# Small vectors of the input factor on VectorE instead of GpSimd, the weight-column product placed later, and new priorities

## The chip, the cores and the metric

The kernel runs on one core of a Trainium2 chip. The metric is device time in microseconds (us) of one execution; the time before is the median of three runs. One further execution was taken by the profiler, and all rows of the profile below come from it.

## The reference

The input `x` has 2048 rows of 1024. The output mixes two branches with a gate for each row:

```
g = sigmoid((x * gate_w).sum(-1))
a = irfft2(rfft2(x) * (w_r + 1j*w_i))          # a spectral filter over rows and columns
dt = exp(log_dt);  Lam_bar = exp(dt * Lam)      # Lam = Lambda_re + 1j*Lambda_im, 1024 states
B_bar = ((Lam_bar - 1) / Lam)[:, None] * (B_re + 1j*B_im)
h_t = Lam_bar * h_{t-1} + B_bar x_t             # a complex recurrence over the 2048 rows
b = 2 * Re(h @ C.T) + x * Dskip
out = g * a + (1 - g) * b
```

The factor `(Lam_bar - 1) / Lam`, times 2, is the "input factor". It is a complex number for each state: `cr` and `ci` in the kernel.

## The kernel before, in words

Five engines work: TensorE (PE), ScalarE (ACT), VectorE (DVE), GpSimd (POOL) and the DMA queues, above all SyncE's (SP).

The rows come in as 16 tiles of 128 and are turned on PE (`turn`, L476), so that columns lie on partitions (`xT`, four chunks `c` of 512 rows). DVE forms sums and differences of the column halves (`halves`), PE and ACT the reflected part (`xps`, L509 and L511).

The spectral branch then has these steps: `fd`, a transform along columns (L650, L655; copy to SBUF on ACT, L661); `s1`, the first half of the transform along rows (L670, copy L673, a store to DRAM called turn 1); `s2w`, the second half and the product with the weights (L761, copy L764, products on DVE, L767); `is1`, `is2` and `idft` back again (L780, L799, L814). Each runs over 16 tiles. One column of the weights needs a correction: `load_Wc` fetches its pieces, element by element (L693); `fixup_w` makes the weight-column product on PE (L702 to L704) and copies it (L706); `fixup` joins it with the first column of the turn-1 data (`Bcol`, L713 and L719).

The recurrence branch handles 8 blocks `jb` of 128 states and 4 chunks. `bu` multiplies `xT` with the turned matrix B (`psu`, L872), ACT copies this into `h` (L875), DVE rotates it with a table of cosines and sines `cs` (`rot`, L840 to L846), runs the real recurrence as a scan (L884) and, in `rot_out`, rotates back with a table `pn` that also holds the input factor (L840 to L844). `table` makes both tables for a block on ACT and DVE (L619 to L634): its last two ACT instructions (L629, L630) multiply by `ci`, and L631 and L634 on DVE use `cr` and `-cr`. The matrix B of blocks 1 to 7 is turned by DMA (`load_BT`, L859, two buffers).

The output stage `yout` multiplies `h` with C (`ps_y`, L931) and adds the skip term (L938). For row tiles below 12, ACT scales the result (L946) and a DMA issued from POOL adds it to the spectral branch (L947), which `unfold` has put together on DVE (L915, L919); the last four tiles are joined on DVE (L954).

The vectors for the states come from five small rows (`vec8`), turned on PE into `vecT`, 128 x 8 each. From them ACT and DVE make `dt`, the decay `r_sb`, the angle `tht` reduced to one turn `rr2`, and its sine and cosine `sn2`, `cs2` (L544 to L557). In the kernel before, 13 small POOL instructions and four on DVE then make `lbr`, `lbi` and the input factor `cr`, `ci`, `ncr`, and two more on POOL make `ns2`, used where the recurrence passes from chunk to chunk.

The order on every engine is fixed when the program is built. A planner (`Plan.run`) takes all operations with their dependencies, a duration written beside each one, and a key; going forward in its own model of time, it gives each engine the operation that could start first, and among those that could start together the one with the smallest key. A buffer slot also has to be free: PSUM has four slots, the buffers of B two. Some kinds of buffer are given out only in the order in which they were declared, those of B among them. Durations in the plan are `us` arguments such as 0.2 for a small DVE instruction and 0.7 for a small POOL one; a DMA lands in the plan after 0.8 + its duration + 1.4. The keys are written with constants `K_...`:

```
KB = lambda p, cc: K_T0 + K_TB * (p + 0.5 * cc) + K_TL * (p >= 12) + K_TM * (p >= 14)   # psu
KD = lambda p: KB(p, 0) + K_D + K_KR * p + K_D1 * turns[p][1]                           # rotation and scan
KF = lambda j: K_F0 + K_F * j                                                            # fd
KW = lambda b: K_W0 + K_W * b                                                            # s2w
tabs[jb] = table(jb, K_TAB0 if jb == 0 else KB(p, 0) - K_TAB)
load_BT(jb, KB(max(p - 2, 0), 0) + K_BT)
```

`p` runs over 16 turns, a turn being one block and two chunks. The copy of `psu` on ACT has the key of `psu` plus `K_KA`. The result of the plan is a fixed order; at run time each engine works it off and waits wherever something is late.

Of the kernel before, what the change touches and what calls it, by code (L numbers as in the profile page):

```python
# [12 lines left out]
ALU = mybir.AluOpType  # L13
# [10 lines left out]
P = 128  # L24
# [273 lines left out]
def kernel(  # L298
# [17 lines left out]
    nc = tc.nc  # L316
# [66 lines left out]

    U = 0.216
    A2 = nc.scalar.activation
    K_T0 = -22.17
    K_TB = 61.63
    K_D = 1206.47
    K_O = -1656.09
    K_TAB0 = 405.37  # L390
    K_TAB = -79.77
    K_F0 = 60.42
    K_F = 11.71
    K_W0 = -27.89
    K_W = 37.7
    K_WI = -461.38
    K_I0 = -5003.33
    K_I = 60.06
    K_ID = -162.81
    K_CT = 644.51  # L400
    K_FIX = -1360.15
    K_R1 = 3.77
    K_R2 = 2542.1
    K_RS = 59.87
    K_Y = -2627.1
    K_YS = 416.09
# [132 lines left out]
    lbr, lbi, nr, t_a, t_b, t_c, t_d, cr, ci, ncr = [
        small(n) for n in ("lbr", "lbi", "nr", "t_a", "t_b", "t_c", "t_d", "cr", "ci", "ncr")]  # L540
    sv = lambda key, fn, r, w: dve(key, 0.2, fn, r=[(i,) for i in r], w=[(i,) for i in w])
    sa = lambda key, fn, r, w, t=None: act(key, 0.22, fn, r=[(i,) for i in r], w=[(i,) for i in w], table=t)
    sg = lambda key, fn, r, w: pool(key, 0.7, fn, r=[(i,) for i in r], w=[(i,) for i in w])
    sa(1, lambda: A2(out=dt, in_=ldt, func=ACT.Exp), ["vecT"], ["dt"], "exp")  # L544
    sv(2, lambda: V.tensor_mul(out=are, in0=dt, in1=lre), ["dt", "vecT"], ["are"])

# [9 lines left out]
    sa(3, lambda: A2(out=sn2, in_=rr2, func=ACT.Sin, scale=TWO_PI), ["rr2"], ["sn2"], "sin")  # L556
    sa(3, lambda: A2(out=cs2, in_=kk2, func=ACT.Sin, scale=-TWO_PI, bias=chpi), ["kk2", "chpi"], ["cs2"], "sin")  # L557
    cTC, sTC = cs2[:, 1, :], sn2[:, 1, :]
    sv(4, lambda: V.tensor_mul(out=den, in0=lre, in1=lre), ["vecT"], ["den"])
    sv(4, lambda: V.tensor_mul(out=den2, in0=lim, in1=lim), ["vecT"], ["den2"])  # L560
    sv(4, lambda: V.tensor_add(out=den, in0=den, in1=den2), ["den", "den2"], ["den"])
    sv(4, lambda: V.reciprocal(out=inv, in_=den), ["den"], ["inv"])
    sg(4, lambda: G_.tensor_mul(out=lbr, in0=r_sb, in1=cs2[:, 0, :]), ["r", "cs2"], ["lbr"])  # L563
    sg(4, lambda: G_.tensor_mul(out=lbi, in0=r_sb, in1=sn2[:, 0, :]), ["r", "sn2"], ["lbi"])
    sg(4, lambda: G_.tensor_scalar_add(out=nr, in0=lbr, scalar1=-1.0), ["lbr"], ["nr"])
    sg(4, lambda: G_.tensor_scalar_mul(out=inv, in0=inv, scalar1=2.0), ["inv"], ["inv"])
    sg(4, lambda: G_.tensor_mul(out=t_a, in0=nr, in1=lre), ["nr", "vecT"], ["t_a"])
    sg(4, lambda: G_.tensor_mul(out=t_b, in0=lbi, in1=lim), ["lbi", "vecT"], ["t_b"])
    sg(4, lambda: G_.tensor_add(out=cr, in0=t_a, in1=t_b), ["t_a", "t_b"], ["cr"])
    sg(4, lambda: G_.tensor_mul(out=cr, in0=cr, in1=inv), ["cr", "inv"], ["cr"])  # L570
    sg(4, lambda: G_.tensor_mul(out=t_c, in0=lbi, in1=lre), ["lbi", "vecT"], ["t_c"])
    sg(4, lambda: G_.tensor_mul(out=t_d, in0=nr, in1=lim), ["nr", "vecT"], ["t_d"])
    sg(4, lambda: G_.tensor_sub(out=ci, in0=t_c, in1=t_d), ["t_c", "t_d"], ["ci"])
    sg(4, lambda: G_.tensor_mul(out=ci, in0=ci, in1=inv), ["ci", "inv"], ["ci"])
    sg(4, lambda: G_.tensor_scalar_mul(out=ncr, in0=cr, scalar1=-1.0), ["cr"], ["ncr"])
    sg(5, lambda: G_.tensor_copy(out=ns2[:, :, 1], in_=sTC), ["sn2"], ["ns2b"])
# [119 lines left out]
    def fixup_w(key):  # L696
        vps = psum([P, 2, 2, 32], "vps2")

        def f():
            for e in range(2):  # L700
                for i, M in enumerate(((MR, MM), (MN, MR))[e]):
                    mm(vps.t[:, e, i, 1:32], lhsT=fix(M, 0), rhs=Wc[:, e, 1:32], start=True, stop=True)  # L702
# [87 lines left out]
    def is2(bp, key):  # L790
        Cq = tile_of([P, 2, K], BF16, "Cq", "Cq")
        dma(key - K_DM, 0.95, lambda: nc.sync.dma_start(out=Cq.t, in_=t2_v[bp]), r=[("t2", b) for b in range(16)], w=[(Cq,)], issue=0.49)
        psz = psum([P, 4, 2, P], "ps_is2")

        def f():
            for kc in range(4):
                par, half = divmod(kc, 2)
                for gg in range(2):
                    mm(psz.t[:, kc, gg, :], lhsT=Cq.t[:, gg, 256 * half + par:256 * (half + 1):2],  # L799
                       rhs=TI_sb.t[:, bp, :], start=True, stop=True)  # L800
        pe(key, 0.65, f, r=[(Cq,), (TI_sb,)], w=[(psz,)])
        ZT = tile_of([P, 4, 2, P], BF16, "ZT", "ZT")
        act(key, 1.01, lambda: nc.scalar.copy(out=ZT.t, in_=psz.t), r=[(psz,)], w=[(ZT,)])  # L803
        return ZT
# [248 lines left out]
```

## Time and profile before

| what | value |
|---|---|
| median of three runs | 327.17 us (326.19 to 328.23) |
| the profiled execution | 326.46 us |
| its span | 324.6 us |
| PE busy | 307.5 us, 95% |
| DVE busy | 284.1 us, 88% |
| ACT busy | 204.7 us, 63% |
| POOL busy | 36.1 us, 11% |

The span is the time from the first to the last instruction of the profiled execution, and 1.86 us of its own time lie around it. A share of busy time is a mean over stages: ACT has little to do in the last 120 us and is full before. A line of the order of time gives the start, the length, the engine, the source line, what is written and read, and in brackets how long the engine was idle before and what ended this.

### The profile page before, as it was taken

To read this page: it belongs to the slowest core of one execution; us is meant where nothing else is said; L and a number is where in the kernel's file an instruction comes from. 1 tells how busy PE (TensorE), PEld (TensorE's weight loads), DVE (VectorE), ACT (ScalarE), POOL (GpSimd) and SP (SyncE) were. 2 spreads that over 40 slices of the span, in tenths; PEclk is the share of its full clock that TensorE was granted. 3 is DMA by queue.
4 is the path that set the end of the run, shared out by engine and by line. 5 is a ranking of instruction groups with operands and counts; after the bars stand their busy time and mean duration, and the time that the engine had idled before them with its cause. 6 is when DMAs were issued, how large, how long until landed. Compare 5 with 4: busy or idle time off the path is not lost.

```text
span 324.6 us, 5143 instructions
## 1 busy us (share of the span) xinstructions
PE 307.5 (95%) x1836; PEld 165.8 (51%) x1869; DVE 284.1 (88%) x439; ACT 204.7 (63%) x280; POOL 36.1 (11%) x47
## 2 busy tenths in 40 slices
PE   5978899999999999999999999999999999999994
PEld 5644665665444444444476566545444444554442
DVE  3999699999999999999899999999999999904114
ACT  3698699999899999989999998304000222131000
POOL 1137300000000000000000000000000444534000
PEclk9999999999999999999999999999999999999999
DMA  7969326997979999985889999770000787896203
GB/s 227 398 156 68 65 98 175 229 223 187 212 194 292 249 294 298 218 225 100 221 195 216 283 243 274 168 269 17 0 0 2 130 179 174 182 175 124 77 0 129
DMA packets 79409, 56.51 MB, mean 174 GB/s; under 512 B 49684, under 2 KB 65428, under 8 KB 79384
## 3 DMA queue, kind: packets, MB, share of 16 engines
q1 hardware_dynamic: 75848, 53.03, 62.8%
q0 software_dynamic: 3456, 3.15, 8.8%
q8 instruction: 14, 0.23, 0.3%
q14 instruction: 11, 0.09, 0.1%
q10 hardware_dynamic: 80, 0.01, 0.0%
HBM read 28.38 MB, written 16.79 MB: 139 GB/s over the span
## 4 chain that ended last, share of the span: by engine, by line
PE 54%; DVE 18%; ACT 16%; DMA 5%; issue 3%; POOL 3%; DVEq 0%; ACTq 0%
PE psu L872 24%; PE ps_y L931 15%; DVE h L884 7%; DMA ga<-y 4%; DVE h L841 3%; ACT h L875 3%; POOL lbr L563 2%; PE ps_id L814 2%; DVE su L840 2%; PE pt L476 2%; DVE h L842 2%; PE ps_fd L650 2%; PE ps_s L670 2%; PE ps_s L761 2%; PE ps_is L780 2%
## 5 line engine op out<-in xcount | busy, mean ns | idle before, releaser
L872 PE MATMUL psu<-xT,BTs 128*128 128x512 bf16 x498 | 115.8, 379 | 2.8 <-ACT G_all L673 0.5
L931 PE MATMUL ps_y<-CT,h 128*128 128x512 bf16 x499 | 112.7, 379 | 1.5 <-ACT y L946 0.8
L872 PEld LDWEIGHTS <-BTs 128*128 128x128 bf16 x512 | 49.6, 98 | 59.1 <-issue 2.7
L931 PEld LDWEIGHTS <-h 128*128 128x128 bf16 x512 | 49.3, 98 | 57.2 <-issue 1.1
L884 DVE TENSOR_TENSOR_SCAN h<-r_sb,carry,h 128x512 bf16<-128x512 f32 x48 | 60.0, 1272 | 0.0
L946 ACT ACTIVATE y<-ps_y,omg 128x512 f32<-128x512 f32 x24 | 15.7, 685 | 69.4 <-PE ps_y L938 32.8
L947 POOL DMA_DIRECT2D ga<-y x24 | 21.3, 1290 | 241.7 <-DVE ga L919 235.7
L875 ACT CAST h<-psu 128x1024 bf16<-128x1024 f32 x32 | 33.3, 1044 | 0.9 <-PE psu L872 0.6
L842 DVE TENSOR_TENSOR h<-h,su 128x1024 bf16<-128x1024 bf16 (+1 forms) x40 | 23.1, 576 | 0.2
L841 DVE TENSOR_TENSOR h<-h,pn 128x1024 bf16<-128x1024 bf16 (+1 forms) x24 | 20.7, 862 | 0.1
L840 DVE TENSOR_TENSOR su<-h,pn 128x1024 bf16<-128x1024 bf16 (+1 forms) x24 | 20.6, 857 | 0.0
L841 DVE TENSOR_TENSOR h<-h,cs 128x2048 bf16<-128x2048 bf16 x16 | 19.6, 1223 | 0.4
L840 DVE TENSOR_TENSOR su<-h,cs 128x2048 bf16<-128x2048 bf16 x16 | 19.3, 1206 | 0.0
L884 DVE TENSOR_TENSOR_SCAN h<-r_sb,h 128x512 bf16<-128x512 f32 x16 | 18.9, 1210 | 0.0
L819 ACT ACTIVATE M_all<-ps_id,gA 128x1024 bf16<-128x1024 f32 x14 | 16.6, 1235 | 2.7 <-PE ps_id L814 2.7
L764 ACT CAST h<-ps_s 128x1024 bf16<-128x1024 f32 x16 | 15.8, 1023 | 0.6 <-remote 0.5
L784 ACT CAST h<-ps_is 128x1024 bf16<-128x1024 f32 x16 | 15.6, 1016 | 0.0
L803 ACT CAST M_all<-ps_is 128x1024 bf16<-128x1024 f32 x14 | 15.3, 1127 | 0.2 <-PE ps_is L799 0.2
L954 DVE SCALAR_TENSOR_TENSOR o<-ps_y,omg,ga 128x1024 bf16<-128x1024 f32 (+1 forms) x5 | 5.3, 1070 | 11.5 <-issue 9.7
L814 PE MATMUL ps_id<-G_all,M_all 128*128 128x256 bf16 x112 | 14.1, 273 | 0.5 <-ACT M_all L803 0.5
L919 DVE TENSOR_TENSOR ga<-G_all 128x512 bf16<-128x512 bf16 x16 | 6.0, 420 | 9.5 <-DMA out_dram<-ga 9.5
L476 PE MATMUL pt<-ident,xn 128*128 128x128 bf16 x128 | 10.0, 242 | 4.0 <-DMA xn<-in_A_x_dram 3.5
(141 smaller groups left out, 413.5 us busy)
## 6 DMA issues: line engine op xcount, KB each, us to landing
xn<-in_A_x_dram SPq DMA_DIRECT2D x16, 256.0 KB, 4.9
h<-turn_scratch SPq DMA_DIRECT2D x16, 256.0 KB, 5.3
turn_scratch<-h SPq DMA_DIRECT2D x16, 256.0 KB, 2.9
ga_scratch<-M_all SPq DMA_DIRECT2D x14, 256.0 KB, 4.3
M_all<-ga_scratch SPq DMA_DIRECT2D x6, 512.0 KB, 4.4
ga<-y POOLq DMA_DIRECT2D x24, 128.0 KB, 5.9
out_dram<-ga SPq DMA_DIRECT2D x12, 256.0 KB, 2.1
turn_scratch<-M_all SPq DMA_DIRECT2D x11, 256.0 KB, 4.9
```

Of the source, the lines that this page charges most:

```text
L476: nc.tensor.transpose(out=pt.t[:, j8, :], in_=src()[:, P * j8:P * (j8 + 1)], identity=ident)
L764: act(key, 1.01, lambda: nc.scalar.copy(out=X2.t, in_=ps2.t), r=[(ps2,)], w=[(X2,)])
L814: mm(pz.t[:, at, :], lhsT=ZT.t[:, 2 * par + half, c, :], rhs=Gi_sb[:, par, half, c, :], start=(half == 0), stop=(half == 1))
L819: act(key, 1.11, lambda: A2(out=eo.t, in_=pz.t, func=ACT.Copy, scale=gA[:, bp:bp + 1]), r=[(pz, 0), (pz, 1), ("gA",)], w=[(eo,)])
L840: dve(key, w, lambda: nc.vector.tensor_mul(out=sv(), in0=src()[:, ::-1], in1=bc(1)), r=sitem + [titem(1)], w=[(su,)])
L841: dve(key, w, lambda: nc.vector.tensor_mul(out=dst(), in0=src(), in1=bc(0)), r=sitem + [titem(0)], w=ditem)
L842: dve(key, h, lambda: nc.vector.tensor_add(out=dst()[:, 0], in0=dst()[:, 0], in1=sv()[:, 0]), r=[(su,)] + r0, w=r0)
L872: mm(psu.t[:, ri, :], lhsT=BT.t[:, ri, db, :], rhs=xT[c][:, db, :], start=(db == 0), stop=(db == 7))
L875: act(kb[cc] + K_KA, 1.01, lambda cc=cc, psu=psu: nc.scalar.copy(out=g()[:, :, cc, :], in_=psu.t), r=[(psu, 0), (psu, 1)], w=ui(cc) + ([(" ...
L884: dve(kd, 1.25, lambda cc=cc, ri=ri, carry=carry: nc.vector.tensor_tensor_scan(out=g()[:, ri, cc, :], data0=rb, data1=g()[:, ri, cc, :], i ...
L931: mm(psy.t[:, 512 * dh:512 * (dh + 1)], lhsT=hbuf[jb // 4].t[:, jb % 4, ri, P * tb:P * (tb + 1)], rhs=CT[pc].t[:, ri, jb % 2, 512 * dh:512 ...
L947: dma(key - 1, 1.3, lambda cols=cols, y32=y32: nc.gpsimd.dma_start(out=ga.t[:, tb % 2, cols], in_=y32.t, accum_op=ALU.add), r=[(y32,)] + [ ...
```

## The change

The products that make the input factor are written with pairs: `cr` and `ci`, real and imaginary part, lie beside each other in one tile, and most instructions handle both. All run on DVE, so that POOL has no part in them. `fixup_w` is called after the loop of `s1`, gets a key of its own, and waits for the turn-1 store of tile 8. The planned duration of the `is2` product goes from 0.65 to 0.46. All key constants have new values, and the small vectors get an offset `K_SM`.

```
-    K_T0 = -22.17
-    K_TB = 61.63
-    K_D = 1206.47
-    K_TAB0 = 405.37
-    K_TAB = -79.77
-    K_F0 = 60.42
-    K_F = 11.71
-    K_W0 = -27.89
-    K_W = 37.7
-    K_R2 = 2542.1
-    K_BT = 425.36
-    K_UN = 2960.8
-    K_KA = -0.82
-    K_WC = 261.15
+    K_T0 = 91.34
+    K_TB = 75.5
+    K_D = 1883.45
+    K_TAB0 = -249.3
+    K_TAB = -891.13
+    K_F0 = 225.83
+    K_F = 11.93
+    K_W0 = -3238.17
+    K_W = 5.91
+    K_R2 = 2615.95
+    K_BT = -266.03
+    K_UN = 3245.96
+    K_KA = 503.92
+    K_KR = -45.15
+    K_WC = 148.64
+    K_FW = -2495.45
+    K_SM = -5128.56
...
-    sv = lambda key, fn, r, w: dve(key, 0.2, fn, ...)
-    sa = lambda key, fn, r, w, t=None: act(key, 0.22, fn, ...)
-    sg = lambda key, fn, r, w: pool(key, 0.7, fn, ...)
+    cs2, sn2 = trig[:, 0], trig[:, 1]
+    sv = lambda key, fn, r, w: dve(key + K_SM, 0.2, fn, ...)
+    sa = lambda key, fn, r, w, t=None: act(key + K_SM, 0.22, fn, ...)
...
-    sv(4, lambda: V.tensor_mul(out=den, in0=lre, in1=lre), ...)
-    sv(4, lambda: V.tensor_mul(out=den2, in0=lim, in1=lim), ...)
-    sv(4, lambda: V.tensor_add(out=den, in0=den, in1=den2), ...)
-    sv(4, lambda: V.reciprocal(out=inv, in_=den), ...)
-    sg(4, lambda: G_.tensor_mul(out=lbr, in0=r_sb, in1=cs2[:, 0, :]), ...)
-    sg(4, lambda: G_.tensor_mul(out=lbi, in0=r_sb, in1=sn2[:, 0, :]), ...)
...
-    sg(4, lambda: G_.tensor_mul(out=ci, in0=ci, in1=inv), ...)
-    sg(4, lambda: G_.tensor_scalar_mul(out=ncr, in0=cr, scalar1=-1.0), ...)
-    sg(5, lambda: G_.tensor_copy(out=ns2[:, :, 1], in_=sTC), ...)
-    sg(5, lambda: G_.tensor_scalar_mul(out=ns2[:, :, 0], in0=sTC, scalar1=-1.0), ...)
+    lam = vecT[:, 0:2, :]
+    two = lambda v: v[:, None, :].to_broadcast([P, 2, 8])
+    cr, ci = co[:, 0, :], co[:, 1, :]
+    sv(4, lambda: V.scalar_tensor_tensor(out=sq, in0=lam, scalar=0.5, in1=lam, op0=ALU.mult, op1=ALU.mult), ...)
+    sv(4, lambda: V.tensor_add(out=inv, in0=sq[:, 0, :], in1=sq[:, 1, :]), ...)
+    sv(4, lambda: V.reciprocal(out=inv, in_=inv), ...)
+    sv(4, lambda: V.tensor_mul(out=lb, in0=trig[:, :, 0, :], in1=two(r_sb)), ...)
+    sv(4, lambda: V.tensor_scalar_add(out=lb[:, 0, :], in0=lb[:, 0, :], scalar1=-1.0), ...)
+    sv(4, lambda: V.tensor_mul(out=lb, in0=lb, in1=two(inv)), ...)
+    sv(4, lambda: V.tensor_mul(out=m1, in0=lb, in1=lam), ...)
+    sv(4, lambda: V.tensor_mul(out=m2, in0=lb, in1=lam[:, ::-1, :]), ...)
+    sv(4, lambda: V.tensor_add(out=cr, in0=m1[:, 0, :], in1=m1[:, 1, :]), ...)
+    sv(4, lambda: V.tensor_sub(out=ci, in0=m2[:, 1, :], in1=m2[:, 0, :]), ...)
+    sv(4, lambda: V.tensor_scalar_mul(out=ncr, in0=cr, scalar1=-1.0), ...)
+    sv(5, lambda: V.tensor_copy(out=ns2[:, :, 1], in_=sTC), ...)
+    sv(5, lambda: V.tensor_scalar_mul(out=ns2[:, :, 0], in0=sTC, scalar1=-1.0), ...)
...
-        pe(key, 0.6, f, r=[("Wc", n) for n in range(8)] + [(TF_sb,)], w=[(vps,)])
+        pe(key, 0.6, f, r=[("Wc", n) for n in range(8)] + [(TF_sb,), ("t1", 8)], w=[(vps,)])
...
-        pe(key, 0.65, f, r=[(Cq,), (TI_sb,)], w=[(psz,)])
+        pe(key, 0.46, f, r=[(Cq,), (TI_sb,)], w=[(psz,)])
...
-    fixup_w(60)
     X1 = fd(0, KF(0))
     for j in range(16):
         nxt = fd(j + 1, KF(j + 1)) if j + 1 < 16 else None
         s1(j, X1, KF(j + 1) + 1)
         X1 = nxt
+    fixup_w(K_FW)
     fixup(K_FIX)
```

More of the change, by code (lines that the diff above doesn't have):

```diff
@@ L533, in small @@
         return cpool.tile([P] + list(shape), FP32, name=n)
-    V, G_ = nc.vector, nc.gpsimd
-    dt, are, r_sb, den, den2, inv = [small(n) for n in ("dt", "are", "r_sb", "den", "den2", "inv")]
-    tht, kk2, rr2, sn2, cs2 = [small(n, (2, 8)) for n in ("tht", "kk2", "rr2", "sn2", "cs2")]
+    V = nc.vector
+    dt, are, r_sb, inv, ncr = [small(n) for n in ("dt", "are", "r_sb", "inv", "ncr")]
+    tht, kk2, rr2, sq, lb, m1, m2, co = [small(n, (2, 8)) for n in ("tht", "kk2", "rr2", "sq", "lb", "m1", "m2", "co")]
+    trig = small("trig", (2, 2, 8))
     ns2 = small("ns2", (8, 2))
[L539 to L543, printed above, removed]
+    cs2, sn2 = trig[:, 0], trig[:, 1]
+    sv = lambda key, fn, r, w: dve(key + K_SM, 0.2, fn, r=[(i,) for i in r], w=[(i,) for i in w])
+    sa = lambda key, fn, r, w, t=None: act(key + K_SM, 0.22, fn, r=[(i,) for i in r], w=[(i,) for i in w], table=t)
     sa(1, lambda: A2(out=dt, in_=ldt, func=ACT.Exp), ["vecT"], ["dt"], "exp")
@@ L558 @@
     cTC, sTC = cs2[:, 1, :], sn2[:, 1, :]
[L559 to L576, printed above, removed]
@@ new lines @@
+    sv(4, lambda: V.tensor_mul(out=lb, in0=trig[:, :, 0, :], in1=two(r_sb)), ["r", "cs2", "sn2"], ["lb"])
+    sv(4, lambda: V.tensor_scalar_add(out=lb[:, 0, :], in0=lb[:, 0, :], scalar1=-1.0), ["lb"], ["lb"])
+    sv(4, lambda: V.tensor_mul(out=lb, in0=lb, in1=two(inv)), ["lb", "inv"], ["lb"])
+    sv(4, lambda: V.tensor_mul(out=m1, in0=lb, in1=lam), ["lb", "vecT"], ["m1"])
+    sv(4, lambda: V.tensor_mul(out=m2, in0=lb, in1=lam[:, ::-1, :]), ["lb", "vecT"], ["m2"])
+    sv(4, lambda: V.tensor_add(out=cr, in0=m1[:, 0, :], in1=m1[:, 1, :]), ["m1"], ["cr"])
```

61 lines of the change are left out of this document (33 added, 28 removed).

## The prediction

> **What bounds the kernel now.** I read the busy totals first, then the busy time in stretches of 10 us, then the waits of each engine, then the order of time where the waits lie, and last the end.
>
> ```profile
> PE 307.5 (95%) x1836; PEld 165.8 (51%) x1869; DVE 284.1 (88%) x439; ACT 204.7 (63%) x280; POOL 36.1 (11%) x47
> ```
>
> ```profile
> 10.00:20.00 10.00, 9.04 (x110) 6.82 (x109) 9.82 (x23) 7.55 (x11) 2.57 (x3) 1.00 1.06 375
> 20.00:30.00 10.00, 8.68 (x38) 3.61 (x37) 9.89 (x17) 9.86 (x15) 5.65 (x5) 1.00 0.67 18
> 30.00:40.00 10.00, 7.91 (x59) 5.51 (x61) 7.22 (x9) 5.48 (x8) 5.21 (x9) 1.00 0.49 93
> 40.00:50.00 10.00, 9.41 (x58) 6.08 (x58) 9.97 (x14) 9.97 (x13) 0.00 (x0) 1.00 0.31 106
> ...
> 170.00:180.00 10.00, 9.45 (x79) 6.55 (x79) 9.93 (x13) 10.00 (x12) 0.00 (x0) 1.00 1.04 228
> ...
> 270.00:280.00 10.00, 9.95 (x47) 4.54 (x47) 10.00 (x17) 0.18 (x1) 4.43 (x6) 1.00 0.79 160
> ```
>
> ```profile
> 3.54 3.60 PE L476 MATMUL pt<-ident,xn 128*128 128x128 bf16 x32 [3.54 <-DMA xn<-in_A_x_dram]
> ...
> 319.77 0.61 PE L938 MATMUL ps_y<-diag,xT 128*128 128x128 bf16 x8
> ```
>
> The columns after each stretch are the busy us of PE, PEld, DVE, ACT and POOL, the granted clock (1.00), the DMA share and GB/s. TensorE is idle 324.6 - 307.5 = 17.1 us in all. It starts at 3.5 us and its last product ends at 320.4, 4.2 us before the end, so about 9.3 us is idle inside, and that is all that any reordering can win. The hole is early: 20 to 40 us lacks 1.32 + 2.09 us. After 40 us DVE is as full as PE (10.00 of 10), and around 170 us ACT is too. Three engines are near their limits, so a gain in one counts only if the others come along.
>
> The waits (engine and line, what it waited for, us in total, times, longest):
>
> ```profile
> ACT tt L629 <- POOL ci L574: 4.0, 1, 4.0
> DVE pn L631 <- ACT tt L629: 3.6, 2, 2.7
> PE ps_s L670 <- ACT M_all L661: 1.4, 1, 1.4
> PE vps L702 <- DMA Wc<-in_A_w_i_dram: 0.9, 1, 0.9
> PE ps_y L931 <- ACT y L946: 0.8, 1, 0.8
> PE psu L872 <- ACT G_all L673: 0.5, 1, 0.5
> PE ps_id L814 <- ACT M_all L803: 0.5, 1, 0.5
> PE psu L872 <- ACT M_all L819: 0.4, 1, 0.4
> PE psu L872 <- ACT h L875: 0.4, 1, 0.4
> PEld L719 <- DMA Bcol<-turn_scratch: 0.4, 1, 0.4
> ```
>
> In order of time (start, length, engine and line):
>
> ```profile
> 10.06 0.16 DVE L545 TENSOR_TENSOR are<-dt,vecT 128x8 f32<-128x8 f32 x1
> 10.14 0.16 DVE L547 TENSOR_TENSOR tht<-dt,vecT 128x8 f32<-128x8 f32 x1
> ...
> 18.28 0.21 ACT L556 ACTIVATE sn<-rr 128x16 f32<-128x16 f32 x1
> ...
> 25.62 0.38 ACT L557 ACTIVATE cs<-kk,chpi 128x16 f32<-128x16 f32 x1
> ...
> 26.08 7.52 POOL L563 TENSOR_TENSOR lbr<-r_sb,cs 128x8 f32<-128x8 f32 x1 [4.35 <-ACT cs L557]
> ...
> 35.29 0.20 POOL L574 TENSOR_TENSOR ci<-ci,inv 128x8 f32<-128x8 f32 x1
> ...
> 37.64 1.22 DVE L840 TENSOR_TENSOR su<-h,cs 128x2048 bf16<-128x2048 bf16 x1
> ```
>
> So the early hole is one chain. The cosines come at 26.0, because their ACT instruction (key 3) stood behind the transposes' copies, whose keys are negative. Then POOL takes 7.52 us for one 128x8 product that takes it 0.20 us elsewhere, `ci` is there at 35.5, ACT has stood 4.0 us before `tt` L629, and DVE 2.7 us before `pn` L631. The fd copies (L661) queued behind on ACT, and so `ps_s` L670 and `psu` L872 on PE waited 1.4 and 0.5 us.
>
> **The change, part by part.**
>
> *Small vectors.* Fifteen POOL instructions and four DVE ones go; thirteen DVE ones come. Their price is read from L545 and L547: each lasts 0.16 us, but starts 0.08 us after the one before. DVE gains 13 - 4 = 9 instructions, 9 x 0.08 = 0.72 us; the other end is 9 x 0.16 = 1.44 us. I take 0.72, since these run in a full queue as those two did. It lies on DVE ahead of the halves that fd needs; PE has psu products to do meanwhile. If that cover were gone, it would cost 0.72. Against it stand the 2.7 us that DVE no longer waits for `pn`: its first rotation (L840, 37.64) should come 2.7 - 0.7 = 2.0 us earlier.
>
> The Trainium skill, "VectorE: DVE Perf Modes", section on the TRN2 errata, speaks against such a move: every VectorE instruction on SBUF pays a fixed latency, which its formula puts at (8 + 151)/0.96 = 166 ns here, and many small ones pay it each time. By that the nine would cost 1.5 us and the rotation would come 1.2 us earlier; the 0.16 us lengths agree with it, the 0.08 us steps do not.
>
> *Keys K_SM and K_TAB0.* K_SM = -5128 puts the whole chain, its ACT parts too, ahead of all copies and halves. The chain began at 10.06 with `are`; sines came 8.2 us later only because of what was queued between. I expect `cs` before 18.3 and `ci` by 22, where 35.5 was. Table 0 (K_TAB0 405 to -249) follows at once. The new wait is that DVE itself now stands before `lb` until ACT has made `cs`; behind it in the same queue are the copies of xT and the halves, and behind these fd on PE. DVE had 0.2 us of slack from 10 to 20 us, so lateness there moves fd, but PE still has psu of jb 0. Bounds: 0 to 1.3 us (half of the 2.7 won); I take 0 for the end.
>
> ACT's 4.0 us hole is then used by what is next in its queue (fd copies, the table of jb 1). So `ps_s` 1.4 and `psu` 0.5 on PE go: 1.9 us. Bounds 1.0 and 1.9; I take 1.9, because both waits name the copies queued behind L629.
>
> *The weight-column product.* Removed: its 0.9 us wait on PE for Wc. It is now placed after the eighth turn-1 store has landed. PE's order is written down by the planner, which allows that store 0.8 + 0.85 + 1.4 = 3.05 us.
>
> ```profile
> turn_scratch<-M_all SPq DMA_DIRECT2D x11, 256.0 KB, 4.9
> ...
> 13.71 8.94 SPq L693 DMA_DIRECT2D Wc<-in_A_w_r_dram  x4
> ...
> 26.98 2.12 SPq L859 DMA_TRANSPOSE BTs<-in_B_B_re_dram  x1
> 29.16 1.29 SPq L859 DMA_TRANSPOSE BTs<-in_B_B_im_dram  x1
> ```
>
> The store lands after 4.9, 1.85 us late, and all later products queue behind the wait. The nearest row of a product placed behind a DMA by the same rule is L719 behind Bcol, 0.4 us of wait. Bounds 0 and 1.85; I take 0.4, net gain 0.5. The twelve products themselves are unchanged.
>
> *BT loads.* K_BT from +425 to -266 puts jb 1's key at 91 - 266 = -175, below every x tile; but its buffer may be taken only after BTb[0] (the slots are taken in order), by which time x is issued. So the two transposes go on SP before TF and TK, or G too, and before the Wc loads instead of behind them: issued near 12 to 16 us instead of 27.0 to 30.5. G, TF and Wc go 2.1 + 1.3 = 3.4 us later; fd and s1 need G and TF only after 34 us, so 0. It gives PE psu work for 30 to 41 us that it lacked; that is the cover for fd's later start, counted at 0 (0 to 1.0, the rest of the early hole).
>
> *The other keys.* The order in each stage is set by differences, which I compared. fd 226 to 405 against psu 91 + 75.5 p: nearly the old place. s2w and is1, is2 and idft stay ahead of psu. Rotations to chunks 2 and 3 stay behind most scans (2616 on, the last scan's key is 2906). New is K_KA = +504: psu's copy on ACT goes behind all fd and s1 copies. I hold this at 0 and carry it as a rival. With ACT some 4 us ahead, the three waits of PE for ACT near 165 to 185 us (0.5, 0.4, 0.4) should shrink: bounds 0 and 1.3. I take 1.3, the whole of it, since each is a third of what ACT is ahead or less.
>
> **The sum.** 1.9 + 0.5 + 1.3 = 3.7 us for PE. DVE must follow:
>
> ```profile
> 277.20 0.68 DVE L844 TENSOR_TENSOR h<-su,h 128x1024 bf16<-128x1024 bf16 x1
> ...
> 281.24 0.61 PE L938 MATMUL ps_y<-diag,xT 128*128 128x128 bf16 x8
> ```
>
> The last rotation ends at 277.9; PE then uses it in the eight products before 281.24 (about 1.7 us), from 279.5. So PE has 1.6 us over DVE, and DVE comes 2.0 earlier: PE can win 3.6 at most without new waits. I take 3.6. The profiled execution took 326.46 us (span 324.6), 0.71 under the median of 327.17, inside the runs' 326.19 to 328.23. It becomes 326.46 - 3.6 = 322.9; from the median 323.6, which is the forecast, 1.1% below. About 1% is what a measurement here can tell from no change, 3.3 us.
>
> **The rivals.**
>
> *A. Given back at the end.* Output tiles leave PSUM through ACT into buffers that a POOL-issued addition must empty, and these additions wait for the unfold on DVE; PE already waited 0.8 us there (`ps_y` L931).
>
> ```profile
> 253.67 6.46 DMA ga<-y
> 260.21 0.69 ACT y L946
> ...
> 261.77 5.71 DMA ga<-y
> ```
>
> If PE reaches the tiles 3.6 us earlier and the unfold does not, since its key rose from 2961 to 3246 against scans that end at 2906, then PE waits for the same additions. For: two such flights lay on the chain that ended last. Against: DVE comes 2.0 earlier. Price 2.0 to 3.6, so 326.4.
>
> *B. Slower: copies of psu starve PE.* There are four PSUM tiles. In the fd stage (about 38 to 77 us) ACT makes 32 fd and s1 copies, about 0.90 us apart, 29 us, for which PE does 16 x (0.87 + 0.43) = 20.8 us of products. If psu's copies (keys 595 on) get no turn against keys of 226 to 417, two or more tiles are stuck and PE loses up to 29 - 20.8 = 8.2 us there.
>
> ```profile
> 60.36 1.04 ACT L673 CAST G_all<-ps_s 128x1024 bf16<-128x1024 f32 x1
> 61.26 1.05 ACT L661 CAST G_all<-ps_fd 128x1024 bf16<-128x1024 f32 x1
> ...
> 58.34 0.60 PE L650 MATMUL ps_fd<-G_all,xpm 128*128 128x256 bf16 x4
> 58.78 0.60 PE L655 MATMUL ps_fd<-G_all,xpm 128*128 128x256 bf16 x4
> 59.22 0.38 PE L670 MATMUL ps_s<-M_all,TF_sb 128*128 128x512 bf16 x1
> ```
>
> Time 327.17 - 3.6 + 8.2 = 331.8. It decides from a loss above 3.6 + 3.3 = 6.9 us for over 1% slower. For: ACT is full in that stage. Against: s1's copy needs s1's product, which needs fd's copy, so ACT has gaps in which psu is next; and where the spectral copies already went first (170 to 180 us) PE lost only 0.55 in 10.
>
> *C. More than forecast.* If the new order also fills most of what is left of the 9.3 us, 6.5 us goes: 320.7. Against: DVE would have to win 4.9.
>
> *D. The change does nothing* to the end, since DVE's 0.7 us and the late store eat the gain: 327.2, counted with A.
>
> **How the numbers follow.** Forecast 0.46 (own range 321.8 to 325.4, two thirds of it under 323.9, since 3.6 is the DVE limit and the order itself may add), A with D 0.24, B 0.20, C 0.10. Faster by over 1%: 0.10 + 0.32 = 0.42. Within 1%: 0.14 + 0.24 = 0.38. Slower: 0.20. The range 319.8 to 330.5 takes in C, A and the milder half of B, and leaves out some 0.16.
>
> **What would show it.** Right: no POOL product after the start, `ci` by 22 us; ACT's 4.0 us and DVE's 2.7 us waits gone; first L840 near 35.6; PE busy over 19 of the 20 us from 20 to 40; the weight-column product between s1 products with a wait below 0.5. A is right if PE's wait before `ps_y` L931 near 260 grows to 3 us; B if PE falls below 9 in 10 between 40 and 80 us while ACT is at 10. The forecast is wrong if the early waits go and the span does not shrink by 2 us, or if `lb` holds DVE for over 1.3 us.

## The result, and the profile after

The changed kernel takes 325.37 us (median of 20 runs, 324.40 to 327.45) against 326.86 us of the kernel before (median of 20, 325.81 to 329.44): ratio 0.9949, 95% interval 0.9929 to 0.9968. That is 1.67 us less by the ratio (1.0 to 2.3), less than half of the 3.6 us that were forecast. The profiled execution has a span of 323.2 us, 1.4 less than before's 324.6.

The busy time of TensorE in stretches of 10 us, columns as in the prediction, shows the early hole filled:

```profile
10.00:20.00 10.00, 8.70 (x105) 6.50 (x103) 9.96 (x31) 8.00 (x13) 0.00 (x0) 1.00 1.17 328
20.00:30.00 10.00, 8.87 (x42) 3.91 (x41) 9.88 (x17) 10.00 (x15) 0.00 (x0) 1.00 0.79 101
30.00:40.00 10.00, 10.00 (x61) 6.20 (x60) 9.86 (x14) 8.81 (x13) 0.00 (x0) 1.00 0.34 53
40.00:50.00 10.00, 9.93 (x67) 6.82 (x65) 10.00 (x14) 10.00 (x12) 0.00 (x0) 1.00 0.49 149
```

From 20 to 40 us TensorE is idle for 1.13 us instead of 3.41, and from 40 to 50 for 0.07 instead of 0.59. Against that, 10 to 20 us loses 0.34, by a new wait at 17.7 us (below). The early stage gives 2.28 + 0.52 - 0.34 = 2.46 us.

Two late stretches, first before, then after:

```profile
160.00:180.00 20.00, 18.92 (x165) 13.38 (x167) 19.93 (x31) 20.00 (x24) 0.00 (x0) 1.00 0.96 224
180.00:200.00 20.00, 19.41 (x151) 12.86 (x152) 19.88 (x29) 20.00 (x29) 0.00 (x0) 1.00 1.06 263
260.00:280.00 20.00, 19.07 (x94) 8.84 (x95) 20.00 (x32) 3.44 (x5) 7.95 (x10) 1.00 0.83 171
```

```profile
160.00:180.00 20.00, 18.10 (x162) 12.56 (x159) 19.97 (x33) 19.98 (x24) 0.00 (x0) 1.00 0.99 236
180.00:200.00 20.00, 19.22 (x147) 12.00 (x145) 19.86 (x30) 18.88 (x26) 0.00 (x0) 1.00 1.04 265
260.00:280.00 20.00, 20.00 (x101) 9.28 (x99) 20.00 (x32) 1.26 (x2) 7.04 (x8) 1.00 0.80 157
```

From 160 to 200 us TensorE is idle for 2.68 us instead of 1.67: 1.0 us is lost where 1.3 was to be won. Around 267 us the wait for an output tile's copy is gone, 0.93 us won that no term of the sum held. Together 2.46 - 1.01 + 0.93 = 2.4 us. Before's trace lacks 33 matmul records, so such differences of busy time are a little uncertain; the last product of TensorE is the better witness:

```profile
317.81 0.61 PE L936 MATMUL ps_y<-diag,xT 128*128 128x128 bf16 x8
```

It ends at 318.42 us, 1.96 earlier than before. From there to the end 4.78 us pass instead of 4.22, with the same work on VectorE between (the last row of VectorE ends 1.5 us after TensorE in both), so the difference lies in the last stores of one execution.

What TensorE still waits for in the changed kernel (us in total, times, longest):

```profile
...
PE pt L478 <- ACT xT L481: 1.3, 2, 1.1
PE psu L870 <- ACT M_all L513: 1.1, 1, 1.1
PE ps_id L812 <- ACT G_all L801: 0.9, 2, 0.6
PE ps_id L812 <- ACT M_all L801: 0.8, 1, 0.8
PE psu L870 <- ACT G_all L817: 0.6, 1, 0.6
PE psu L870 <- ACT M_all L817: 0.4, 1, 0.4
```

The waits for `ps_s`, for Wc and for `ps_y` are not in it. Two early waits are new. At 17.7 us `pt` waits 1.1 us for a copy of `xT` that now stands on ScalarE behind a table load and the small sines and cosines (15.0 to 16.7 us, where K_SM puts them). By this trace it is a price of the early place; no run took it away. At 25.9 us psu waits 1.1 us. The other rows lie between 163 and 197 us. The chain that filled the early hole, in order of time:

```profile
12.55 1.55 SPq L857 DMA_TRANSPOSE BTs<-in_B_B_re_dram  x1
14.15 4.33 SPq L857 DMA_TRANSPOSE BTs<-in_B_B_im_dram  x1
...
16.43 0.29 ACT L558 ACTIVATE trig<-kk,chpi 128x16 f32<-128x16 f32 x1
...
18.61 0.17 DVE L572 TENSOR_TENSOR co<-m 128x8 f32<-128x8 f32 x1
...
23.58 0.75 ACT L627 ACTIVATE tt<-tf,co 128x512 f32<-128x512 f32 x1
...
36.77 1.22 DVE L838 TENSOR_TENSOR su<-h,cs 128x2048 bf16<-128x2048 bf16 x1
```

The cosines come at 16.4 instead of 25.6 us, `ci` at 18.8 instead of 35.5, ScalarE's scaling of the table starts at 23.6 without a wait, and the B loads of block 1 run at 12.6 to 18.5 us.

### The profile page after: what moved, and what is told of

Its sections match the earlier page's. It is cut to its first block, busy times and chain, and to the rows that moved or that the text cites. A ratio compares the mean times of both kernels' runs of the same rounds, so it can differ in the third digit from the quotient of the medians.

```text
span 323.2 us, 5180 instructions
## 1 busy us (share of the span) xinstructions
PE 308.9 (96%) x1869; PEld 165.3 (51%) x1869; DVE 285.2 (88%) x448; ACT 204.6 (63%) x280; POOL 22.5 (7%) x32
## 4 chain that ended last, share of the span: by engine, by line
PE 62%; ACT 17%; DMA 9%; DVE 6%; issue 3%; SPq 2%; DVEq 0%; ACTq 0%
PE ps_y L929 34%; PE psu L870 14%; PE ps_id L812 2%; DMA wA<-in_A_w_r_dram 2%; PE ps_y L936 2%; ACT h L782 2%; ACT M_all L801 2%; PE ps_fd L648 2%; PE ps_fd L653 2%; PE ps_s L668 2%; DVE wA L765 1%; ACT h L873 1%; DMA Bcol<-turn_scratch 1%; DMA wB<-in_A_w_i_dram 1%; DMA xn<-in_A_x_dram 1%
## 5 line engine op out<-in xcount | busy, mean ns | idle before, releaser
L873 ACT CAST h<-psu 128x1024 bf16<-128x1024 f32 x32 | 32.4, 1022 | 3.0 <-PE psu L870 3.0
L882 DVE TENSOR_TENSOR_SCAN h<-r_sb,h 128x512 bf16<-128x512 f32 x16 | 18.8, 1208 | 0.0
L817 ACT ACTIVATE M_all<-ps_id,gA 128x1024 bf16<-128x1024 f32 x12 | 13.6, 1162 | 1.0 <-PE ps_id L812 1.0
L801 ACT CAST M_all<-ps_is 128x1024 bf16<-128x1024 f32 x12 | 12.6, 1060 | 1.3 <-PE ps_is L797 1.3
L812 PE MATMUL ps_id<-G_all,M_all 128*128 128x256 bf16 x96 | 12.4, 273 | 0.8 <-ACT M_all L801 0.8
```

What stands on the lines that cost most here:

```text
L812: mm(pz.t[:, at, :], lhsT=ZT.t[:, 2 * par + half, c, :], rhs=Gi_sb[:, par, half, c, :], start=(half == 0), stop=(half == 1))
L873: act(kb[cc] + K_KA, 1.01, lambda cc=cc, psu=psu: nc.scalar.copy(out=g()[:, :, cc, :], in_=psu.t), r=[(psu, 0), (psu, 1)], w=ui(cc) + ([(" ...
L882: dve(kd, 1.25, lambda cc=cc, ri=ri, carry=carry: nc.vector.tensor_tensor_scan(out=g()[:, ri, cc, :], data0=rb, data1=g()[:, ri, cc, :], i ...
```

## The experiments

Two kinds of kernel were run. In the first, each engine's order is written down, as the kernel before has it or as the changed kernel has it, and one thing is moved in it. In the second, the planner draws up the order anew. All come from one source with other line numbers: L988 is the product psu and L991 its copy; L587 the copy of xps, L777 that of fd, L786 the s1 product, L818 the weight-column product; L919 and L935 are the copies of the inverse stage (the changed kernel's L801 and L817), L915 and L930 its products ps_is and ps_id; L960 is the last step of a rotation; L1035 the additions of the unfolding, L1063 the additions that POOL issues, L1047 and L1054 the output products and L1062 their copy; L745 and L747 are the table's scaling by `ci` and its use in `pn`. The kernel before, measured again beside them, took 326.9 to 327.5 us, so kernels are compared by their ratios to it.

| kernel | us | ratio to before | 95% interval |
|---|---|---|---|
| bo_dve | 326.36 | 0.9982 | 0.9961 to 1.0004 |
| bo_vps | 328.31 | 1.0042 | 1.0023 to 1.0060 |
| bo_both | 326.21 | 0.9976 | 0.9957 to 0.9994 |
| bo_both_unf | 326.09 | 0.9964 | 0.9943 to 0.9985 |
| bo_both_unf2 | 325.67 | 0.9940 | 0.9913 to 0.9967 |
| ao_pool | 324.84 | 0.9945 | 0.9918 to 0.9971 |
| ao_pool_late | 330.23 | 1.0097 | 1.0065 to 1.0129 |
| ao_dve_late | 328.54 | 1.0039 | 1.0013 to 1.0066 |
| ao_diag | 324.83 | 0.9929 | 0.9907 to 0.9952 |
| ao_light | 324.01 | 0.9894 | 0.9868 to 0.9920 |
| oldkeys_newcode | 355.51 | 1.0858 | 1.0829 to 1.0888 |
| newkeys_is2_065 | 327.36 | 1.0003 | 0.9985 to 1.0020 |

### The edits in the order of before

**bo_dve**: the small vectors alone.

```diff
 order of before
-POOL: lbr, lbi, nr, inv, t_a, t_b, cr, ... ncr, ns (15), behind the cosines
+DVE:  ns, lb, lb-1, lb*inv, m1, m2, cr, ci, ncr (10), behind the last subtraction before the cosines
```

> The order of the kernel before is kept on every engine, instruction by instruction; only the small vectors are made in pairs on VectorE, the ten that need the cosine directly behind the subtraction that DVE did at 26.9 us. Theory 1 (the early chain is what the change removes, and the gain reaches the end): ACT's wait of 4.0 us before L629 and DVE's 2.7 us before L631 go, the first rotation comes near 35.6 instead of 37.6, PE wins 1.4 + 0.5 us near 40, and since nothing else moves the whole rest shifts: 1.5 to 2.0 us faster, ratio near 0.995. Theory 2 (the gain is one of the new order, the small vectors were hidden): the early waits shrink, later waits grow by as much, ratio 1.000 within 0.001.

```profile
PE ps_y L1047 <- ACT y L1062: 1.5, 1, 1.5
PE vps L818 <- DMA Wc<-in_A_w_i_dram: 1.5, 1, 1.5
```

The waits of 1.4 us for `ps_s` and of 0.5 for psu are gone or down to 0.2, 1.7 us won. But Wc is now waited for 1.5 us instead of 0.9, since TensorE reaches that product earlier and the load lands when it did, and the output tile's copy at 267 us 1.5 instead of 0.8. So 1.3 of 1.7 is given back. The ratio is 0.18% below 1, and its interval takes in 1. This is rival A of the prediction, in the old order.

**bo_vps**: the weight-column product alone.

```diff
 order of before
-PE vps, ACT Vc   (at 30.6 us)
+PE vps, ACT Vc   directly ahead of zps
```

> The order of the kernel before is kept; only the twelve small weight-column products and their copy are moved to just before the first-column products (L719, 85 us). POOL still makes the small vectors. Theory 1: PE's 0.9 us wait for Wc goes, but fd then meets the same late ACT (L629), so the gain is 0 to 0.9 us, ratio 0.997 to 1.000. Theory 2: 1.000 within 0.001.

TensorE in order of time (the bracket holds the idle time before, and what ended it), then busy time and granted clock (the seventh number) in two stretches:

```profile
39.00 0.59 PE L786 MATMUL ps_s<-M_all,TF_sb 128*128 128x512 bf16 x2 [2.72 <-ACT M_all L777]
...
41.41 1.06 PE L786 MATMUL ps_s<-G_all,TF_sb 128*128 128x512 bf16 x2
```

```profile
38.00:40.00 2.00, 1.00 (x7) 0.75 (x7) 1.97 (x2) 2.00 (x4) 0.00 (x0) 1.00 0.00 0
40.00:42.00 2.00, 2.00 (x9) 1.13 (x8) 1.97 (x4) 2.00 (x3) 0.00 (x0) 0.53 0.00 0
```

The 0.9 us at Wc turns into 1.3 us more in front of `ps_s`, because POOL's slow `ci` still sets when that is fed. On top of it the clock falls to half from 40.1 us, 1.1 us after the wait has ended, and a like pair of s1 products takes 1.06 instead of 0.59 us. Both theories missed: the edit alone costs 0.42%.

**bo_both**: the two together.

> The order of the kernel before with both edits at once: small vectors on VectorE and the weight-column products at 85 us. Theory 1: the early waits of PE, 0.9 + 1.4 + 0.5 = 2.8 us, go together, and 2.0 to 2.8 us reach the end, ratio 0.991 to 0.994, as good as the changed kernel (0.995) or better, with no new priorities. Theory 2: the changed kernel stays ahead; this one is at 0.998 to 1.000.

```profile
PE ps_fd L766 <- DVE xpm L574: 0.7, 2, 0.5
...
PE ps_y L1047 <- ACT y L1062: 1.1, 1, 1.1
```

0.24% is won, close to what the second theory says. What stands in the way is VectorE's later halves (`xpm`, 0.7 us) and again the end.

**bo_both_unf** and **bo_both_unf2**: is the wait at the end what eats the gain?

```diff
 VectorE's order of bo_both
 bo_both_unf:
-ga additions 2 to 4 of the first pair at 248.2 to 251.2 us
+ga additions 2 to 4 of the first pair at 233.8 us
 bo_both_unf2, that and:
-pq and ga, six additions of the second pair, between rotations at 252.7 to 261 us
+the six together ahead of the rotation at 253.3 us
```

> Both edits in the kernel before's order, as in the earlier run of it (326.2 us, ratio 0.9976), and now three additions of the first unfolded pair (`ga`, on VectorE at 248.2 to 251.2 us there) placed at 234 us. Theory 'given back at the end': there TensorE waits 1.1 us at 267 us for an output tile's copy, which waits for a buffer, which waits for a POOL-issued addition, which waits for those three. Then the wait falls under 0.3 us and the time by about 1.1 us to 325.1, ratio near 0.994. Rival 'VectorE sets the end': three additions of 0.42 us ahead of rotations make TensorE wait for the rotations, 326.2 or up to 327. Rival 'the next wait takes its place': the y wait goes, another of 1 us appears, 326.2.

> Both edits in the order of before, and the first two unfolded pairs' additions on VectorE earlier: three of the first pair at 234 us (which alone left the wait at 267 us as it was, since the copy there waits for the POOL additions at 260 us, and these for the second pair), and the six of the second pair together at 253.3 to 256 us instead of 252.7 to 261. Theory 'given back at the end': POOL's additions come some 5 us earlier, TensorE's wait of 1.1 us at 267 us falls under 0.3, the time falls by 0.8 to 1.1 us to 325.2 (ratio near 0.9945, as the change). Rival 'VectorE sets the end': the rotation behind the six comes 1.3 us later and TensorE waits for it instead, 326.2 or more.

The first one missed: the wait stayed at 1.1 us, since the copy at 267 us hangs on POOL's second group of additions, at 260.6 us, and that on the second pair. In bo_both_unf2 that group is issued at 255.9:

```profile
255.92 3.52 POOL L1063 DMA_DIRECT2D ga<-y  x4 [17.15 <-issue]
```

```profile
268.36 11.61 PE L1047 MATMUL ps_y<-CT,h 128*128 128x512 bf16 x52 [0.21 <-DVE h L960]
```

Now 0.2 us is left, and that is for a rotation. The ratio is 0.9940, as the whole change has it (0.9949). So rival A's wait was real: the trace shows it gone, the span falls from 324.3 us in bo_both to 323.6, and the two edits in the old order then give what the change gives. The ratios of bo_both and bo_both_unf2 alone do not separate the two, since their intervals overlap.

### The engine, or the place

**ao_pool**: the changed kernel's order with the fifteen POOL instructions back, at the early place.

```diff
 order of the changed kernel
-DVE:  ns, lb, ... ncr (10) at 16.6 to 18.9 us
+POOL: the 15 instructions of before, behind the cosines at 16.8 us
```

> The order of the changed kernel is kept; only the small vectors go back to POOL, where they start behind the cosine at 16.7 us. Theory 1 (it is the late input factor that costs): one of the fifteen POOL products stands still for some 5 to 8 us again, ci comes at 25 to 29 us instead of 18.7, ACT waits before L627 (23.6 us) for 2 to 5 us, and 1 to 2 us of the gain are lost: ratio 0.998 to 1.002. Rival: the early place alone is what counts; POOL is done by 23 us and the ratio stays near 0.995.

```profile
17.86 0.20 POOL L680 TENSOR_TENSOR lbr<-r_sb,cs 128x8 f32<-128x8 f32 x1
...
19.75 0.74 POOL L691 TENSOR_TENSOR ci<-ci,inv 128x8 f32<-128x8 f32 x1
```

`lbr` took 7.52 us before and takes 0.20 here, and the time is the changed kernel's (0.9945 against 0.9949). The second theory holds: it is the early place (K_SM) that counts, not VectorE.

**ao_pool_late** and **ao_dve_late**: the cosines late again.

```diff
 order of the changed kernel, small vectors on POOL or on DVE
-ACT cs at 16.4 us, small vectors behind it
+ACT cs and small vectors directly ahead of ACT's scaling of the table (23.6 us)
```

> The changed kernel's order with the small vectors on POOL (as fast as the changed kernel when the cosines come at 16.8 us), and now cosines and small vectors only right before the table's scaling by `ci` (about 23.9 us). Theory 'place, not engine': the cosines then fall among VectorE's products of two operands in SBUF (23.0 to 27 us), the first POOL product takes several us instead of 0.20, `ci` comes near 30, ScalarE waits 4 us or more, and TensorE loses 1 to 3 us: 326 to 328. Rival 'length of the chain only': each product 0.20 us, `ci` at 27.5, ScalarE waits some 3 us, the time within 0.5 us of after's 325.4.

> The changed kernel's order with cosines and small vectors (on VectorE, in pairs, as in the change) only right before the table's scaling by `ci` (about 23.9 us). Theory 'place, not engine': VectorE waits some 0.3 us for the cosines, the ten small instructions take 1.1 to 1.4 us, ScalarE waits about 1.3 us for `ci`; the time within 0.5 us of after's 325.4, and below the same place on POOL by 1 us or more. Rival 'the early place is all': as slow as on POOL in that place.

On POOL:

```profile
23.88 0.57 POOL L680 TENSOR_TENSOR lbr<-r_sb,cs 128x8 f32<-128x8 f32 x1 [6.23 <-ACT cs L674]
```

```profile
27.30 0.72 ACT L745 ACTIVATE tt<-tf,ci 128x512 f32<-128x512 f32 x1 [3.50 <-POOL ci L691]
```

```profile
29.58 9.75 PE L988 MATMUL psu<-xT,BTs 128*128 128x512 bf16 x31 [4.93 <-ACT M_all L587]
```

```profile
30.00:32.00 2.00, 2.00 (x6) 0.70 (x5) 2.00 (x4) 2.00 (x4) 0.00 (x0) 0.50 0.41 1
```

On VectorE, the ten instructions' first and last, and TensorE behind them:

```profile
24.19 0.17 DVE L649 COPY ns<-trig 128x8 f32<-128x8 f32 x1
...
25.36 0.17 DVE L648 TENSOR_SCALAR ncr<-co 128x8 f32<-128x8 f32 x1
```

```profile
27.79 8.75 PE L988 MATMUL psu<-xT,BTs 128*128 128x512 bf16 x31 [2.65 <-ACT M_all L587]
```

Both missed. No POOL product took several us: the first four took 0.48 to 0.57, the others 0.20, so ScalarE waited 3.5 us for the length of the chain. Yet the times are far beyond what either theory gave: 330.2 and 328.5. The wait on TensorE is 4.9 us (2.65 with VectorE) where the changed kernel has 1.1, and behind it the 32 products of psu, of which these traces hold 31, take 9.75 us (8.75). In the changed kernel the same ones take 7.07:

```profile
25.89 7.07 PE L870 MATMUL psu<-xT,BTs 128*128 128x512 bf16 x32 [1.13 <-ACT M_all L513]
```

So 3.8 us of wait and 2.7 of a slow clock (1.5 and 1.7) make 6.5 us (3.2); the spans, 329.0 and 326.7, are 5.8 and 3.5 above the changed kernel's. In this place VectorE beats POOL by 1.7 us, which is what the change of engine is worth when the chain is late.

### The late waits

**ao_diag** and **ao_light**: what ScalarE does from 160 to 200 us.

```diff
 ScalarE's order of the changed kernel
 ao_diag:
-eight diag copies at 178.9 to 192.5 us
+eight diag copies behind the last copy of the inverse stage (205 us)
 ao_light, that and:
-two scalings of the last table at 173.0 and 175.4 us (pn on DVE at 173.9 and 176.8)
+two scalings at 205 us (pn on DVE at 208.7)
-psu copy at 195.1 us, then the copy for ps_id
+the copy for ps_id, then the psu copy
```

> The changed kernel's order with one thing moved: the eight small ScalarE copies that make the diagonal (some 0.3 us each, 2.4 us, at 178.9 to 192.5 us) go behind the last copy of the inverse stage (205 us), where ScalarE stands idle. Theory 'ScalarE is the bound from 160 to 200 us': it is at 10.00 of 10 there, so 2.4 us less work ends TensorE's waits after 179 us (0.78 at 197 us), TensorE idle from 180 to 200 us falls from 0.78 to below 0.3, the time falls by 0.5 to 0.8 us to 324.7; the waits from 163 to 178 us (1.9 us) stay. Rival 'each wait is the length of one copy that the next product needs, whatever the load': waits and time stay as after's, 325.4. Rival 'VectorE sets the end': the waits go and the time does not.

> The changed kernel's order with ScalarE's work put off where TensorE waits for it: besides the eight diagonal copies (moved to 205 us, which alone moved no wait), the two scalings of the last table (at 173.0 and 175.4 us, 1.6 us, used only after 206 us) go to 205 us with their two VectorE instructions behind them, and one copy of psu (195.1 us) goes behind the copy of the inverse stage that TensorE waits for at 197 us. Theory 'ScalarE's local order': each late wait of TensorE is a copy that queued behind an instruction nobody needed yet. Then the waits of 0.57 us at 177 and 0.78 at 197 us go, those of 0.63 at 163 and 0.40 at 167 us stay, TensorE gains about 1.3 us and the time falls to 324.0, ratio near 0.9905. Rival 'VectorE sets the end': TensorE's waits go and others for VectorE come, 325.2. Rival 'one copy's length': the waits stay, 325.2.

Busy time in ao_diag, then in ao_light:

```profile
180.00:200.00 20.00, 19.11 (x150) 12.53 (x151) 19.89 (x29) 17.12 (x19) 0.00 (x0) 1.00 1.11 257
```

```profile
160.00:180.00 20.00, 18.39 (x163) 12.85 (x164) 19.93 (x32) 19.29 (x21) 0.00 (x0) 1.00 0.98 226
180.00:200.00 20.00, 19.83 (x153) 12.85 (x153) 19.86 (x30) 17.56 (x20) 0.00 (x0) 1.00 1.06 253
```

In ao_diag ScalarE has 1.8 us less to do from 180 to 200 us and TensorE waits as before (0.89 idle), so that "ScalarE is full there" is not the cause of the waits. The time went to 324.83 us, near the expected 324.7, but the ratios (0.9929 and the change's 0.9949) are not apart by their intervals, and the waits that this fall was to come from did not change. In ao_light, which moves what stands directly ahead of the copies that TensorE waits for, 180 to 200 us lacks only 0.17 us, and the whole stretch from 160 lacks 1.78 instead of 2.68. The wait of 0.8 us at 197 us is gone; that at 177 shrank from 0.57 to 0.35 only. At 197 us ScalarE and TensorE stood so in the changed kernel, then in ao_light:

```profile
195.07 1.03 ACT L873 CAST h<-psu 128x1024 bf16<-128x1024 f32 x1
195.97 1.03 ACT L801 CAST M_all<-ps_is 128x1024 bf16<-128x1024 f32 x1
...
197.06 1.05 PE L812 MATMUL ps_id<-G_all,M_all 128*128 128x256 bf16 x8 [0.78 <-ACT M_all L801]
```

```profile
194.01 2.11 ACT L919 CAST M_all<-ps_is 128x1024 bf16<-128x1024 f32 x2
...
195.07 2.16 PE L930 MATMUL ps_id<-G_all,M_all 128*128 128x256 bf16 x16
```

The copy for `ps_id` no longer stands behind the copy of psu, and TensorE's products follow without a gap.

The time goes to 324.01, ratio 0.9894, whose interval does not touch the change's; the expected 324.0 was met. It is the fastest kernel of this study, 0.55% (1.8 us) below the changed kernel by the two ratios, of which the profile shows 1.0 in the span. VectorE's last rotation and TensorE's tile that uses it stand so in it:

```profile
278.29 0.68 DVE L960 TENSOR_TENSOR h<-su,h 128x1024 bf16<-128x1024 bf16 x1
```

```profile
281.02 0.61 PE L1054 MATMUL ps_y<-diag,xT 128*128 128x128 bf16 x8
```

The eight products before this row take 1.7 us, from 279.3, and the rotation ends at 278.97. Only 0.3 us is left, so by this trace VectorE is the next limit; no run tested that.

### The keys and the planned durations

**oldkeys_newcode** and **newkeys_is2_065**: the planner draws up the order anew.

```diff
 oldkeys_newcode: the changed code
-all new keys
+all old keys; K_SM = 0, K_FW = 60
 newkeys_is2_065: the changed kernel
-pe(key, 0.46, f, r=[(Cq,), (TI_sb,)], w=[(psz,)])
+pe(key, 0.65, f, r=[(Cq,), (TI_sb,)], w=[(psz,)])
```

> The changed code with the old keys (and the two new keys at values in the middle of the old ones: none extra for the small vectors, 60 for the weight-column product), so that the list is drawn up anew from the old keys. Theory 'keys and durations belong together': the order comes out different in many places, not only in the edited ones; the small vectors stay behind the copies, the transposes for the second block stay late, and the time is above before's, 328 to 345. Rival 'the edits do it by themselves': as both edits in the old order, 326.2, ratio 0.9976.

> The whole change with one planned number back at its old value, the duration of the second inverse product (0.65 instead of 0.46 us); the code and the keys are the changed kernel's. No instruction differs, only the order that the list comes to. Theory 'keys and durations belong together' (old keys with the new code took 355.5 us): a small change of one planned duration moves the inverse stage's products against psu's and ScalarE's copies, TensorE's waits from 160 to 200 us change (2.7 us with 0.46) by a microsecond or more, and the time goes up by 1 to 4 us to 326.5 to 329. Rival 'only the code and the keys count': the same order but for a few neighbours, 325.4, ratio 0.995.

With the old keys, first VectorE in order of time, then busy times:

```profile
55.01 0.75 DVE L747 SCALAR_TENSOR_TENSOR pn<-tf,co,tt 128x512 bf16<-128x512 f32 x1 [17.55 <-ACT tt L745]
```

```profile
40.00:60.00 20.00, 19.84 (x123) 13.13 (x124) 1.50 (x2) 19.99 (x24) 0.00 (x0) 1.00 0.58 160
...
200.00:260.00 60.00, 43.62 (x234) 22.78 (x238) 59.93 (x91) 14.47 (x17) 3.65 (x4) 0.83 0.42 107
```

The new code with the old keys is 8.6% slower than before. The scalings of the first table queue on ScalarE behind fd's copies, and VectorE, whose next instruction needs them, stands 17.5 us. TensorE feels nothing of it then (19.84 of 20). From 200 to 260 us it is idle for 16.4 us, at a mean clock of 0.83; 13.1 us of this are two waits for rotations, 3.1 us are waits for ScalarE's copies. That the rotations are late because VectorE stood at 37 to 55 us is argued from the order, and no run changed this alone.

With one planned number put back, the busy times of the inverse stage are:

```profile
160.00:180.00 20.00, 17.35 (x151) 11.73 (x149) 19.93 (x33) 19.99 (x24) 0.00 (x0) 1.00 0.84 209
180.00:200.00 20.00, 17.88 (x139) 11.12 (x137) 19.86 (x29) 17.51 (x24) 0.00 (x0) 1.00 1.00 235
```

```profile
PE ps_is L915 <- DMA M_all<-turn_scratch: 1.9, 2, 1.3
```

The early stage is the changed kernel's (1.12 us idle from 20 to 40), but from 160 to 200 us 4.77 us are idle instead of 2.68, and the whole gain is gone: ratio 1.0003. The list now places inverse products where their loads have not landed. So without the 0.46 the rest of the change wins nothing, and no instruction is altered by it. The new keys came together with the 0.46; whether other keys would do as well with 0.65 was not run.

## Why the prediction was right and where it was wrong

**The size: less than half.** Of 3.6 us forecast, 1.67 came. At 325.4 us the time lies at the upper end of the forecast's own range, 321.8 to 325.4, and well inside the wide one, 319.8 to 330.5. By its own sign the forecast failed: it was to be wrong "if the early waits go and the span does not shrink by 2 us", and the early waits went and the span shrank by 1.4.

**Early terms: right in mechanism, in their sum partly by luck.** The forecast had 1.9 for the two waits and 0.5 for the weight-column product, 2.4 us; the trace has 2.46. The three waits named (1.4, 0.5 and 0.9 us) went, and the 0.4 us set against them for the late store did not come. But two new waits of 1.1 us each came, at 17.7 and 25.9 us, which the sum put at nothing, and small waits of `pt` and `xps` for copies of `xT` at 16 to 22 us, 1.7 us in before, went almost wholly, which it did not hold either. `cs` (16.4, asked for before 18.3), `ci` (18.8, before 22), the B loads at 12 to 16 and the wait of the weight-column product (none over 0.2) came as said; TensorE over 19 of 20 us was missed by little (18.87). At 25.9 us psu waits for a copy that stands behind the table's scalings on ScalarE. It is the wait removed at 38 us in a smaller form.

**Small vectors: right in size.** In ao_dve_late the ten behind the cosines take from 24.19 to 25.44, 0.125 us each; the forecast lay between 0.08 and 0.16 and took 0.08. No wait of TensorE in the changed kernel names these instructions, so the price was covered. But the sum took the engine for a part of the gain, and ao_pool shows that the early place alone carries it.

**First rotation: mis-sized.** It came 0.87 us earlier, at 36.77, not 2.0. The 2.7 us that VectorE no longer waits were used for other things ahead of it, the halves and the second table. The last rotation did not come earlier at all: it ends at 278.36 us against 277.9 before. TensorE won 2.0 and still had 1.7 us of room, as the eight products that use it start at 280.1, and these 3.7 us are close to the limit of 3.6. That is luck: VectorE did not lead by 2.0 us, and the new order puts this tile 0.6 us later. The changed kernel did not reach it; ao_light nearly does.

**Late waits: this step failed, with the wrong sign.** The prediction took 1.3 us, "since each is a third of what ACT is ahead or less". The measurement is 1.0 us lost. A lead of ScalarE at 40 us is not carried to 165 us. bo_dve and bo_both show this with the order kept: the early waits for ScalarE go, and from 160 to 200 us TensorE is idle for 1.67 and 1.68 us, as before (1.67). There a copy can't start before its product has ended, and how long TensorE waits beyond that is decided by the instruction that stands directly ahead of the copy. ao_light shows it at 197 us and in part at 177 us; no run moved the waits at 163 and 167 us, and for these it is argued. (The copy waited for at 163 us starts at 161.98, behind a table load of 1.28 us and one instruction of the last table.) The prediction compared keys by their differences and found the order "nearly the old place"; newkeys_is2_065 shows that one planned duration, which the prediction did not price, moves this stage by 2.1 us. The term should have been 0 with bounds on both sides: against before, the runs in the new order lose from 0.1 us (ao_light) to 3.1 us (newkeys_is2_065) in this stage, and none gains.

**End: better than taken.** Rival A did not come, though its mechanism is real: bo_dve shows the wait grow to 1.5 us in the old order, and bo_both_unf2 takes it away. In the new order POOL issues its first additions at 227.4 us (250.7 in bo_both), and the wait is not there, 0.9 us won. The prediction had only VectorE's lead to set against A; it had not compared when those additions come.

**Rivals.** B is refuted: from 40 to 80 us TensorE is busy for 39.93 of 40. D is refuted too. C came in no run.

Together: of the 3.7 us of the terms, 2.4 early came as forecast, 1.3 late became -1.0, and 0.9 at the end stood for 0. That makes 2.3, and less 0.6 us of the last stores 1.7. The ratio of the medians gives the same 1.7, with an interval from 1.0 to 2.3; the two profiled spans differ by 1.4.

## What to carry to other kernels

When an order is drawn up from priorities and planned durations, code, keys and durations are one thing: new code with old keys cost 8.6%, one planned duration 0.5%. Take a gain early in the program as far as the next wait with a fixed end (a load, a queue of additions) and price that wait too; in the old order 1.3 of 1.7 us went there. For a wait of TensorE look at the one instruction ahead of the copy it needs, rather than at how full that engine is: 1.8 us less work left every wait as it was; three instructions moved on top of it took 0.9 us off the waits, and both together 0.55% off the time.

## What the runs showed of the hardware

A wait of TensorE can cost twice. After idle times of 2.65 (ao_dve_late), 2.72 (bo_vps) and 4.93 us (ao_pool_late) the granted clock fell to 0.5; a pair of products took 1.06 instead of 0.59 us. The fall came 3.4, 3.8 and 3.6 us after the wait had begun, in the first two with products already running again, and it lasted 3.4, 3.4 and 6.8 us. After 1.42 us (before, 38.7 us) and 1.1 us (after, 25.9 us) it stayed at 1.00. The Trainium skill, "TensorE: Matmul & The Clock Gate", section on the HAM clock gate, gives half the clock after an idle window of about 3.4 us. The half agrees with the 0.50 here; the length does not, since 2.65 us was enough in ao_dve_late.

The 7.52 us of one POOL product remain open in part. In ao_pool_late POOL worked beside the same kind of VectorE products and lost some 0.3 us for each of four. The Trainium skill, "SBUF — State Buffer", section "Who interferes with whom", says that a VectorE instruction with two inputs in SBUF holds off a GpSimd one that reads SBUF, by order of issue. Four products of 0.48 to 0.57 us instead of 0.20 agree with that; in before the one product ended at 33.60 us, 0.06 us after VectorE's unbroken run of such products, and so it did in bo_vps (7.52 us again, 33.89 and 33.83). Why it found no turn between the products of that run, when the four in ao_pool_late did, no run here shows.
